# Pooled attention and an MLP on one core: fewer, larger transfers for each head, query rows placed otherwise, and a new order of steps

## The chip, the cores and the metric

The kernel runs on one core of one Trainium2 chip. The metric is the device time of one execution in microseconds (us); the numbers to compare are medians over several executions. All inputs and outputs are float32.

## The reference, cut to what matters

```
q_pool = q.reshape(B, H, S // 2, 2, D).mean(axis=3)            # B 4, H 8, S 1152, D 64
scores = (1 / sqrt(D)) * q_pool @ k.T                           # 576 x 1152 for each head
scores = scores - max(scores, axis=-1)
attn   = exp(scores) / (sum(exp(scores), axis=-1) + 1e-9)
x      = (attn @ v), heads side by side                         # 2304 x 512
h      = x @ w_in                                               # 512 x 2048
out    = max(0.01 * h, h) @ w_out                               # 2048 x 512
```

## The kernel before, in words

There are 32 heads (`hd`) of attention and nine blocks (`i`) of 256 tokens of the MLP. A head goes through these steps, each a function of the kernel:

- `load_q` (line 402), `load_k` (374) and `load_v` (457) fetch its inputs. `load_q` issues four transfers, one for each (x, y) quarter of 144 query rows; all heads share one buffer for them.
- `q_sum` (419, GpSimd) adds the two rows of each pooled pair, `q_tr` (425, TensorE) transposes, `q_hi` (440, ScalarE) and `q_lo` (443, VectorE) split the result into a high and a low part, so that products of reduced precision add up to a full one. Both parts are needed twice, on partitions 0 to 63 and on 64 to 127. For head 0 the engines write all four (x, y) quarters; for all others they write the two with x = y, and `q_dup` (449) copies them to the other partitions with two transfers for the high and two for the low part.
- `qk` (463, TensorE) forms scores with high parts alone, `vmax` (478, VectorE) takes their row maxima, `vneg` (490) reduces and negates them, `m_tr` (493, TensorE) and `m_cp` (499, ScalarE) turn them into a row, and `m_dma` (503) writes this row into partition 0 and into partition 64 of a tile, with one transfer each (head 0: in two halves).
- `qkt` (540, TensorE) forms the transposed scores minus the maxima, `exp` (552, ScalarE) their exponentials, from head 15 on partly after a subtraction by VectorE (`less`, 535). `esum` (559, GpSimd) adds exponentials up and `pv` (573, TensorE) multiplies by v, in two bursts.
- For heads 0 to 12, `r_mm` (584, TensorE) forms the row sums, `r_cp` (613, ScalarE) copies them, `r_fold` (617) spreads them over 96 partitions (four transfers, for head 12 two), `r_inv` (630, VectorE) inverts, `r_row` (641) writes a row to memory, `r_wide` (647) reads it back on all partitions (two transfers). Later heads form the sums on VectorE (`r_tr`, 603) and fold them with four transfers of another shape.
- `scale` (657, GpSimd) multiplies, `x_out` (660) stores the head's share of x with two transfers.

That is 22 transfers for a head of the first dozen. All of them, those of the weights (`w_load` 668, `w_out_dma` 707, `ws_load` 740) and those of the MLP (`x_load` 719, `o_out` 902, `o_mix_out` 876) are issued one after the other by SyncE's queue (SP); a wait there holds all that is behind it. Only `load_q` of head 0 is issued by ScalarE's queue.

The MLP's first product is `l1` (748), its second `l2` (883) for blocks 0 to 3 and `l2s` (833) after that. Its steps are laid between those of the heads: the first `l1` stands in the order between the first `qkt` of head 10 and that of head 11.

All engines run in order, and this order is written out by hand: the string `ORDER` (line 49) has one letter for each step, `FAMILIES` (38) says which function a letter is. `Scheduler.run` (163) goes through it; its model of the engines' times decides which of two engines takes a step that either could, and which buffer it gets, nothing else. TensorE works in four tilings, line 85:

```
TILINGS = {"pv": 1, "r_mm": 2, "qk": 3, "qkt": 3, "m_wide": 3, "k_tr": 3, "q_tr": 3, "m_tr": 3}
```

All else (the MLP's products) has tiling 0, and `r_mm` from head 12 on has that of `pv`.

Of the kernel before, what the change touches and what calls it, by code (L numbers as in the profile page):

```python
# [21 lines left out]
SWITCH = 0.19  # L22
OND = 0.0
ON_DVE = ()
LAT = 0.12
FLIGHTS = 10
PELAT = 0.28
FAST = 4
DEEP = 4
NEAR = 1  # L30
MB = 15
# [18 lines left out]
    "&(!#)*$++++--!&@%F,,(,,)-...!#-!$*.-.-+(.+.)/01A--,2,%-/0F1.*-+..+.,3433A,4-4.#-$2AF3.43.34%--/04313.4.#-4.($%"  # L50
    ")-2F(334.3443*+-A6+A43FG45,,-.34FH..-/!I60.1-55555348343.-24.3)*-+453+.433-,,644()79.-.A./!3#$A%G6H4I8031-3-F4"
    "F.54(533.43-.4&55-:&47-.2!9JF5A3434.:#$;#*+%+6,,$%3334-55;5..7K/)44<A=>34--J6.0.53-559G13H454I<.J&-!A.!?-=G234"
    ".3434-3F4384..>*H#:&/L0++?,16,$;3K(5K%GIHIGJ34K46AAG384)55HIH3323444-7-IJ55<L..9--..6FGJ3-3=4344.>(#:;L*+-+,6,"
    "../5KK$0134%3343!4?45558H<I&A-7L--).9.GH364-*..+-+,,5=>F652I-3.()3JJJ.4!A./4A-0?.18345F3-43.F4-34-34.33-4A..-2"
    "&34..:#743F;(5/&<$F940%314*+33+,4,6:G3A43445K5)HLI3K45#-6$;.-%3*GK=HJ(4I++>.,7,9-.--.J<26.3L!A-.=A4534.33-F544"
    "G/?.H85>!6?013I-.YJ-4557):93.83-44343;-.F2334.-4F&4..AK/KK34343#04<$61%*3FG:555555;H=I+,+GFJ6(H4I)A<3>3G4Y24,#"
    "H$I=-K.37%49--3.6J.?48*-.->6.3G-+,+,5!545LK53344..33/453A?()44A-3H-V8W&4I7X..-039:;.#&1*4-A.L$55(Y+ZZZZZZ,G%<6"
    "2J+H,IJJ!5A[534-.-.&7.3=433K3>FK:44#$K4%6/09Y3314343?4;A4-.L!55)6G*-G++HHII,<.,J625333F54&K34433444ZYZ--=]:LZZ"
    ";ZZZ.>.(Z8-<.-.ZYJG[ZZ?]ZA^Y=.8)555[57/(03133444-HIK623>Y39.GF3]^^4-HI?G64H4L8-5I3..4334A-*4+ZZ555555Z.Z,-#J&+"
    ",-.ZZY$ZYAZJFZ[ZZZ%:FJAF-[../03KK1343-4.72K564-;9].)--^.LG63..43-3434..34!3355:4/5L<LH553I5446Y_G4FFHJI____KG]"  # L60
    "GHIHJI^GGKLLJJKKHHIJI;____55555_JKF0YB#__1_2$%_*3`+<+4ZKZ,,Z_3CZD5ZYZFE[33EEG6G=>AG-H]IYJH_^KIZJ`ZKZZZZ[]Y.H:;"
    "ZZ=YIF_?_-.J>3K^4A5?EZZZZ(GHI[]8!___J-43^K)8-<44VE4W__._.Y(_-.-.=./*__+X+__0,A,133>53___E4&44B#2C`D`3$36%E--.."
    "5554-.633&YYE!?38E#3)&$4EZZZZZZ4E*%Y3+-5ZEZ[+:.ZZ--]4,Y44YA^ZZZZZA,[YYZZY]3.;<.555-.4-..ZAZZ(&Z4-3^B.-[]:55Z/!"
    "^4ZZ_.__01-[34.-.2_]6.CD3_;_^_E)_<4==`533*+6+/E53Y,,5555A4E0143E#4E43E$B%36Y3>555444>2aCD3a?33A4EE-(?86.-)-Z8_"
    "ZY.:.Z!;--345__5.E44ZZ.Z-*&+.+3E(<___./55_A_,0=,31#!`2E3EZZZYY4ZZZ$A44)-[([%33553454-.655.->B-?4C.D.63855YY333"
    ":E4]5E]ZZZ^ZEE335-Z445Z_EE.-[*]&#);+ZZZZZ.!+A.,,44$Z^^/0<=4%1354234_--[.55V5&]63.C^5__D433B_:_EE-.3E>?_;_`3*+W"
    "X6+3,8,A3YY-AEE.#55_E_$%_-<=->-...__YZZZZZY3.-4A-Z4444[__.]B!5ZZ.55(/)^445ZZ_01?-3:-ZZ4[]-..6.52CD5;.<3=`/53E4"
    "4#3(E3E64^3>$%4Y830E!3E142*Y3++3E5,,4655444?AB):CDA345333EE44*+55aE6,;554+-,-8__YY5Z.-53..E-ZZ.ZZZ-.#[-]<$.A_Z"
    "Z-.-a^%ZZZZ._Y[.-&33_=>B_EE]^4(4__?-5)43`4/3.-:4.01.;3-5.5./555234*6<CDE&56(++,3041,3=38EEE!333Y3E4444E2AA>?B)"
    "44456CD35555&3&A#4$3EY3%EE46345Y:8*E+3(E4!-,Z.+,___---Z.A.ZZZ.Z_-.-..[/554#__$%]4_03313YE44-!ZZ4Z2ZZZ;[5555B--"  # L70
    ".5.653.CZ<D_Z]Z3)Y43`5:ZZ^ZEE[533#$E%*=Y4+,+,6E3E(>43?8E344-.AZ_;44YZA5-4.34-..ZZY-A<5-.^Z6/0.-).Z1!2_-V-_.]_."
    "Y^__[]^CD-__34B..`35*/E4+3E43E4+:=&63(;0555515>,,3E4E34E#3A$6442B%5CD-.34-.3A5553E3&45E5!#-.$5-%63.E33E33E?EW<"
    "84:;4)4X44-6-Y44=ZZZ...*/0Z15ZZ++,,33[3B>(555<4?34=2C6DE>?E333E558485E3E)&*4Y:_A54E5+5_,+,_;---...Z]^!ZZ_ZZZ--"
# [27 lines left out]

class Scheduler:
# [33 lines left out]
    def free_slots(self, tag):  # L136

        r = []
        for after, before, slots in self.tags[tag]:
            if (after is None or after in self.done) and before not in self.done:  # L140
                for slot in slots:
                    t = [self.cells[c] for c in slot]
                    if None not in t:
                        r.append((max(t), slot))
        return sorted(r, key=lambda x: x[0])
# [27 lines left out]

    def start(self, s, e, at):
# [11 lines left out]
        free, end = self.free[e], at + s.eng[e]  # L186
        self.free[e] = end
        if e == "PE":
            if at > free + 1.0:
                end = self.free[e] = end + (1.2 if at > 20 else 0.3)  # L190
# [11 lines left out]
        for hold in self.holds.pop(s.key, ()):  # L202
            hold[1] -= 1
            hold[2] = max(hold[2], end)
            if hold[1] == 0:
                for c in hold[0]:
                    self.cells[c] = hold[2] + LAT
        for k, wait in self.after.pop(s.key, ()):
# [4 lines left out]
            elif e == "PE":  # L213
                t = end if "PE" in o.eng else end + 2 * LAT
            else:
                t = end + (PELAT if "PE" in s.eng else LAT)
# [4 lines left out]
def tile_pooled_attention_moe(  # L221
# [40 lines left out]
    def copy(e, out, in_):  # L262
# [18 lines left out]
        "ms": (1, [NQ, 128], F32R, sb),  # L281
# [167 lines left out]
    def q_dup(hd, lo, e):  # L449
        t = f32((ql if lo else qh)[hd])  # L450
# [39 lines left out]
    def vneg(hd, a, b, e):  # L490
        nc.vector.tensor_reduce(out=mng[hd][:, a:b], in_=mx[hd][:, a:b], axis=AX.X, op=ALU.max, negate=True)
# [7 lines left out]
    def m_cp(hd, a, b, e, i):  # L499
        mst[hd] = new("ms", i)  # L500
        nc.scalar.copy(out=mst[hd].rearrange("p (x n) -> p x n", x=2), in_=mtp.pop(hd)[0:NQ, :, :64])

    def m_dma(hd, a, b, e, i=None):
# [3 lines left out]
        src = f32(mst.pop(hd))[a:b]  # L507
# [109 lines left out]
    def r_fold(hd, e, i):  # L617
# [100 lines left out]

    def x_load(i, e, s):
# [5 lines left out]
        n0 = 0  # L725
# [185 lines left out]
    def mmr(*cols):  # L911
        return {"PE": sum(max(0.112, 0.0035 + 0.000436 * c) for c in cols)}

    def mm4(*cols):
        return {"PE": sum(0.01 + 0.00182 * c for c in cols)}

    def trr(n):
        return {"PE": 0.112 * n}

# [23 lines left out]
    for hd in range(NHD):  # L943
# [7 lines left out]
        step(k_tr, hd, eng=trr(NP + 1), deps=[("load_k", hd)] + after("k_tr"), takes=[("tp", [("k_hi", hd), ("k_lo", hd)]), ("ka", [last])])  # L951
# [3 lines left out]
        step(load_q, hd, **(sp(4, 0.3e6, 0.47, 200e3) if hd else dict(eng={"ACT": 4.4})), order=after("load_q"), takes=[("qn", [("q_sum", hd)])])  # L955
# [213 lines left out]
```

## Time and profile before

| | before |
|---|---|
| median of 3 runs | 888.05 us (887.7 to 889.61) |
| the profiled execution's own time | 885.79 us |
| its span, first to last instruction | 884.0 us |
| what lies around the span | 1.79 us |
| mean granted TensorE clock | 0.989 |

The profile shows one execution. Busy times are unions of an engine's instructions; PE is TensorE's matrix products, PEld its weight loads, DVE VectorE, ACT ScalarE, POOL GpSimd, SP SyncE. `L453` is line 453 of the kernel. A row such as `PE L550 ... [1.46 <-DVE stat L488]` says that the engine stood idle for 1.46 us and that an instruction of VectorE's line 488, writing tile `stat`, ended this. PEclk is the granted share of TensorE's full clock. The q after an engine's name means its instruction queue: for SP these are the issues of transfers.

### The profile page before, as it was taken

How to read it: one execution, taken by the hardware profiler on the slowest of the kernel's cores; microseconds unless marked ns; L12 is line 12 of the kernel's file. 1: busy time of each engine (PE TensorE's matmuls, PEld its weight loads, DVE VectorE, ACT ScalarE, POOL GpSimd, SP SyncE). 2: the span in 40 equal slices, each digit the busy share in tenths (PEclk: the TensorE clock that was granted, in tenths of full speed). 3: DMA queues.
4: the chain of work that ended last, by engine and by line, in shares of the span. 5: the costliest groups of instructions: out<-in, count | busy, mean ns of one | idle time of the engine just before them, and what ended most of it. 6: DMA issues, size and time to landing. Idle time of an engine off the chain costs nothing.

```text
span 884.0 us, 19586 instructions
## 1 busy us (share of the span) xinstructions
PE 843.9 (95%) x7492; PEld 678.2 (77%) x7492; DVE 588.3 (67%) x1000; ACT 408.8 (46%) x730; POOL 480.1 (54%) x387
## 2 busy tenths in 40 slices
PE   4999899899999999999999999999999999999997
PEld 2766565666777877686776776787789999999997
DVE  6877677574666776677787778767559985533454
ACT  2566565665556544254446345444433343323231
POOL 2565846685889757576869749857861021004000
PEclk9999999999999999999999999999999999999999
DMA  5666666667786674454464544464547778575641
GB/s 159 181 175 166 181 195 188 196 200 226 212 275 222 203 230 143 116 171 131 141 185 130 152 135 132 134 192 147 175 136 263 263 251 250 152 265 186 206 135 36
DMA packets 105313, 159.85 MB, mean 181 GB/s; under 512 B 23861, under 2 KB 72309, under 8 KB 105221
## 3 DMA queue, kind: packets, MB, share of 16 engines
q1 hardware_dynamic: 104581, 158.32, 59.0%
q8 instruction: 59, 0.97, 0.5%
q10 hardware_dynamic: 640, 0.30, 0.1%
q14 instruction: 33, 0.27, 0.1%
HBM read 131.12 MB, written 17.90 MB: 169 GB/s over the span
## 4 chain that ended last, share of the span: by engine, by line
PE 79%; DVE 7%; DMA 7%; SPq 2%; ACT 2%; issue 1%; POOL 1%; DVEq 0%; ACTq 0%; POOLq 0%
PE banks L758 21%; PE banks L550 14%; PE banks L579 14%; PE banks L849 11%; PE banks L473 5%; PE banks L890 4%; PE banks L891 3%; PE banks L892 3%; DVE stat L488 3%; DMA ws<-wd 2%; PE banks L595 1%; DVE e L538 1%; DMA fold<-rs 1%; PE banks L476 1%; DMA kn<-in_k_dram 1%
## 5 line engine op out<-in xcount | busy, mean ns | idle before, releaser
L488 DVE TENSOR_REDUCE stat<-banks 128x1 f32<-128x1024 f32 (+3 forms) x224 | 217.0, 1005 | 67.0 <-PE banks L473 52.1
L758 PE MATMUL banks<-xb,ws 128*128 128x256 f32 x1344 | 179.1, 286 | 2.0 <-DMA ws<-wd 1.9
L758 PEld LDWEIGHTS banks<-xb,ws 128*128 128x128 f32 x1344 | 167.3, 191 | 13.4 <-issue 7.3
L567 POOL TENSOR_TENSOR sm<-sm,e 128x576 f32<-128x576 f32 x119 | 167.0, 1422 | 6.0 <-ACT e L557 2.6
L550 PE MATMUL banks<-qh,ka 64*128 64x288 f32 x1152 | 138.3, 318 | 6.7 <-DVE stat L488 3.3
L579 PE MATMUL banks<-e,vv 128*64 128x288 f32 x924 | 143.7, 417 | 0.0
L550 PEld LDWEIGHTS banks<-qh,ka 64*128 64x128 f32 x1152 | 94.6, 190 | 35.1 <-DVE stat L488 8.5
L557 ACT ACTIVATE e<-banks 128x576 f32<-128x576 f32 x146 | 90.1, 649 | 55.1 <-PE banks L550 45.9
L579 PEld LDWEIGHTS banks<-e,vv 128*64 128x64 f32 x924 | 70.1, 138 | 43.7 <-issue 8.4
L550 PE MATMUL banks<-ql,ka 64*128 64x288 f32 x576 | 87.7, 295 | 0.0
L538 DVE TENSOR_TENSOR e<-banks,e 128x576 f32<-128x576 f32 x85 | 61.4, 752 | 34.3 <-PE banks L550 26.3
L473 PE MATMUL banks<-ka,qh 64*128 64x512 f32 (+1 forms) x320 | 70.3, 461 | 5.3 <-DMA qh<-qh 2.2
L554 ACT ACTIVATE e<-e 128x576 f32<-128x576 f32 x85 | 56.4, 682 | 21.4 <-DVE e L538 21.1
L423 POOL TENSOR_TENSOR qs<-qn 112x384 f32<-112x384 f32 x32 | 32.2, 1006 | 58.1 <-DMA qn<-in_q_dram 39.5
L771 POOL TENSOR_TENSOR gg<-g,gg 128x512 fp32r<-128x512 f32 x31 | 39.8, 1290 | 43.5 <-ACT gg L263 41.7
L849 PE MATMUL banks<-wo,gg 128*128 128x256 f32 x344 | 63.1, 283 | 0.0
L738 POOL TENSOR_TENSOR xb<-xb 128x1024 fp32r<-128x1024 f32 x7 | 16.7, 2387 | 85.1 <-ACT xb L263 83.2
L550 PE MATMUL banks<-mt,hot 64*128 64x288 f32 x372 | 58.3, 298 | 0.9 <-DMA mt<-ms 0.9
L550 PEld LDWEIGHTS banks<-ql,ka 64*128 64x128 f32 x576 | 56.8, 188 | 0.0
L890 PE MATMUL banks<-wo,gg 128*128 128x512 f32 x124 | 52.1, 420 | 0.7 <-DVE ql L444 0.4
L567 POOL TENSOR_TENSOR sm<-e 128x576 f32<-128x576 f32 x30 | 42.6, 1424 | 18.1 <-ACT e L554 11.7
L658 POOL TENSOR_TENSOR x<-x,rs 128x288 f32<-128x288 f32 x32 | 25.9, 810 | 48.3 <-DMA rs<-rd 35.4
(221 smaller groups left out, 1571.8 us busy)
## 6 DMA issues: line engine op xcount, KB each, us to landing
ws<-wd SPq DMA_DIRECT2D x144, 512.0 KB
vv<-in_v_dram SPq DMA_DIRECT2D x32, 288.0 KB
kn<-in_k_dram SPq DMA_DIRECT2D x32, 288.0 KB
qn<-in_q_dram SPq DMA_DIRECT2D x124, 72.0 KB
raw<-in_moe_w_in_dram SPq DMA_DIRECT2D x16, 512.0 KB
raw<-in_moe_w_out_dram SPq DMA_DIRECT2D x16, 512.0 KB
wd<-ws SPq DMA_DIRECT2D x16, 512.0 KB
rs<-rd SPq DMA_DIRECT2D x64, 72.0 KB
```

The lines of the kernel that those rows point to most:

```text
L473: nc.tensor.matmul(p[:n, x, :KW], lhsT=qh[hd][r, o:o + n], rhs=kh[r, :KW], start=True, stop=True)
L488: nc.vector.tensor_reduce(out=d, in_=p, axis=AX.X, op=ALU.max)
L538: nc.vector.tensor_tensor(out=ex[hd, u], in0=sps.pop((hd, u))[:, :, :HW], in1=m, op=ALU.add)
L550: nc.tensor.matmul(p[:, x, :HW], lhsT=w[r], rhs=m[r, hf * HW:(hf + 1) * HW], start=(n == 0), stop=(n == len(todo) - 1))
L554: nc.scalar.activation(out=ex[hd, u], in_=ex[hd, u], func=AF.Exp)
L557: nc.scalar.activation(out=ex[hd, u], in_=sps.pop((hd, u))[:, :, :HW], func=AF.Exp)
L567: ENG[e].tensor_tensor(out=o, in0=a, in1=b, op=ALU.add)
L579: nc.tensor.matmul(p[64 * hf:64 * hf + 64, :HW], lhsT=vv[hd][:, t, :], rhs=probs(hd, t, hf), start=(t == 0), stop=(t == KT - 1),)
L758: nc.tensor.matmul(p, lhsT=wst[i, f][:, a, c, :], rhs=xx[i][x][:, c, :], start=(n == 0), stop=(n == 3 * KC - 1))
L771: ENG[e].tensor_tensor(out=t[:, 1], in0=gf.pop((i, fp)), in1=f32(t[:, 0]), op=ALU.subtract)
L849: nc.tensor.matmul(o, lhsT=g[i, p][:, a], rhs=w[:, x], start=(p == 0 and n == 0 and half == 0), stop=(p == FH - 1 and n == 2), skip_group_ ...
L890: nc.tensor.matmul(p, lhsT=gh, rhs=wo[f][:, 0], start=(f == hf * FH), stop=False)
```

## The change

- `load_q` takes the query rows in another split: row n of a head's 576 pooled rows stood at (x, y, a, p) with n = 288 x + 144 y + 48 a + p and now stands at n = 288 y + 144 x + 48 a + p. One transfer now covers both x, so there are two instead of four. `q_sum` writes with permuted strides to give the old layout. The two middle quarters of the columns of x are thereby exchanged, and `x_load` undoes this: `pieces` cuts a block at quarters of 144 columns, which makes 24 transfers of all nine blocks where there were 12.
- `q_hi` writes all four quarters for every head (128 ScalarE instructions where there were 66); `q_dup` copies only the low part (two transfers, not four).
- `vneg` writes the negated maxima twice, `m_cp` copies 10 rows instead of 5, and `m_dma` writes both partitions with one transfer (head 0 stays as it was).
- `r_fold` of heads 0 to 12 takes both halves in one transfer: two (head 12: one) instead of four (two).
- The model's figures are others (among them one for TensorE's clock), and `ORDER` is a new string: 3709 letters where there were 3678, the difference being 62 more `q_hi` and 31 fewer `q_dup`. Read with `FAMILIES` and `TILINGS`, the old string changes TensorE's tiling 282 times, the new one 249 times: 79 and 73 before head 13's first `qkt`, 203 and 176 from there on.

The strings and most of the model's figures are left out:

```diff
 ORDER = (
-    "&(!#)*$++++--!&@%F,,(,,)-...!#-!$*.-.-+(.+.)/01A--,2,%-/0F1.*-+..+.,3433A,4-4.#-$2AF3.43.34%--/04313.4.#-4.($%"
...
+    "()!#$%*++,++-,,,---@&&&(.)-...*++-!.+.#/()$01*%+++,.--,/++-.FF..23,,-A04.3-(1#4-!.323$..34/440%-.133)A4-(3.4-"
...
     def load_q(hd, e, i):
-        src = q[hd // H, hd % H].rearrange("(x y a p r) d -> x y p a (r d)", x=2, y=2, p=QP, r=2)
+        src = q[hd // H, hd % H].rearrange("(y t p r) d -> y p t (r d)", y=2, p=QP, r=2)
         dma = nc.sync if hd else nc.scalar
-        for x in range(2):
-            for y in range(2):
-                dma.dma_start(out=qraw[64 * y:64 * y + QP, x::2], in_=src[x, y])
+        for y in range(2):
+            dma.dma_start(out=qraw[64 * y:64 * y + QP], in_=src[y])
...
-        a, b = (qraw[:n, :, r * D:(r + 1) * D] for r in range(2))
-        ENG[e].tensor_tensor(out=qs[hd][:n], in0=a, in1=b, op=ALU.add)
+        a, b = (qraw[:n, :, r * D:(r + 1) * D].rearrange("p (x a) d -> p x a d", x=2) for r in range(2))
+        ENG[e].tensor_tensor(out=qs[hd][:n].rearrange("p (a x) d -> p x a d", x=2), in0=a, in1=b, op=ALU.add)
...
-    def q_dup(hd, lo, e):
-        t = f32((ql if lo else qh)[hd])
+    def q_dup(hd, e):
+        t = f32(ql[hd])
...
     def vneg(hd, a, b, e):
-        nc.vector.tensor_reduce(out=mng[hd][:, a:b], in_=mx[hd][:, a:b], axis=AX.X, op=ALU.max, negate=True)
+        out = mng[hd][:, :2 * NQ].rearrange("p (x n) -> p x n", x=2)[:, :, a:b]
+        src = mx[hd][:, a:b].unsqueeze(1).to_broadcast([128, 2, b - a, 2])
+        nc.vector.tensor_reduce(out=out, in_=src, axis=AX.X, op=ALU.max, negate=True)
...
-        src = f32(mst.pop(hd))[a:b]
+        src = f32(mst.pop(hd))
+        if b - a == NQ:
+            nc.sync.dma_start(out=f32(mt[hd])[::64].rearrange("p (i n) -> p i n", n=128), in_=src)
+            return
+        src = src[a:b]
...
-        for hf in range(2):
-            for x in range(parts(hd)):
-                j = 64 * hf + 32 * x
-                src = rss[hd][j:j + 1].rearrange("o (a n) -> o a n", n=RN)
-                nc.sync.dma_start(out=rts[hd][HW // RN * hf:HW // RN * (hf + 1), x], in_=src)
+        for x in range(parts(hd)):
+            src = rss[hd][32 * x:32 * x + 65:64].rearrange("o (a n) -> o a n", n=RN)
+            nc.sync.dma_start(out=rts[hd][:, x], in_=src)
...
+    def pieces(i):
+
+        n0, r = 0, []
+        while n0 < NB:
+            b, at = divmod(i * NB + n0, SP)
+            j, o = divmod(at, HW // 2)
+            n = min(NB - n0, HW // 2 - o)
+            r.append((n0, n, b, (0, 2, 1, 3)[j] * (HW // 2) + o))
+            n0 += n
+        return r
...
-        while n0 < NB:
-            b, o = divmod(i * NB + n0, SP)
-            n = min(NB - n0, SP - o)
+        for n0, n, b, o in pieces(i):
             src = xd[b].rearrange("(c p) n -> p c n", p=128)[:, :, o:o + n]
             nc.sync.dma_start(out=f32(xx[i][1])[:, :, n0:n0 + n], in_=src)
-            n0 += n
...
-        quarters = [(x, y) for x in range(2) for y in range(2) if x == y or hd < NEAR]
+        quarters = [(x, y) for x in range(2) for y in range(2)]
+        lows = [z for z in quarters if z[0] == z[1] or hd < NEAR]
...
-            step(q_dup, hd, 0, **sp(2, 0.15e6, 0.58), deps=high)
-            step(q_dup, hd, 1, **sp(2, 0.15e6, 0.58), deps=low)
-            high, low = [("q_dup", hd, 0)], [("q_dup", hd, 1)]
+            step(q_dup, hd, **sp(2, 0.15e6, 0.58), deps=low)
+            low = [("q_dup", hd)]
```

## Rows read from the trace of the kernel before

**Rows 1.** Busy time by stretch: start:end, length, busy (instructions), PEclk, DMA share, GB/s.
```profile
core 0: us, PE busy (x) PEld busy (x) DVE busy (x) ACT busy (x) POOL busy (x), PEclk, DMA share, GB/s
...
50.00:250.00 200.00, 185.40 (x1936) 129.76 (x1932) 128.27 (x193) 117.42 (x221) 140.00 (x111) 0.97 0.68 197
250.00:650.00 400.00, 395.29 (x3370) 298.54 (x3371) 282.06 (x430) 193.26 (x347) 294.54 (x227) 1.00 0.56 167
650.00:884.00 234.00, 227.12 (x1850) 223.17 (x1846) 141.03 (x322) 76.15 (x121) 29.11 (x29) 1.00 0.60 195
```

**Rows 2.** The same view, first and last of five stretches of 3.41 us.
```profile
65.89:69.30 3.41, 3.41 (x22) 1.86 (x24) 1.94 (x5) 1.50 (x3) 1.00 (x1) 0.50 0.40 124
...
369.67:373.08 3.41, 3.41 (x9) 2.62 (x9) 1.87 (x5) 0.00 (x0) 3.30 (x3) 0.50 0.26 70
```

**Rows 3.** Timeline of PE at either clock: start, length, instruction, count.
```profile
162.25 0.80 PE L550 MATMUL banks<-qh,ka 64*128 64x288 f32 x4
...
163.22 0.80 PE L550 MATMUL banks<-qh,ka 64*128 64x288 f32 x4
...
262.25 0.43 PE L550 MATMUL banks<-qh,ka 64*128 64x288 f32 x4
...
262.78 0.42 PE L550 MATMUL banks<-qh,ka 64*128 64x288 f32 x4
```

**Rows 4.** Timeline of SP's queue, 134 to 140 us.
```profile
134.30 1.18 SPq L453 DMA_DIRECT2D qh<-qh  x2
135.53 0.58 SPq L708 DMA_DIRECT2D wd<-ws  x1
136.16 1.25 SPq L651 DMA_DIRECT2D rs<-rd  x2
137.50 2.62 SPq L407 DMA_DIRECT2D qn<-in_q_dram  x4
```

**Rows 5.** Source views of five lines: duration ns min/median/max, first and last start.
```profile
L407 SPq DMA_DIRECT2D qn<-in_q_dram x124: 312/435/1480, 7.8 to 571.9; - x124
...
L453 SPq DMA_DIRECT2D qh<-qh x62: 461/537/1706, 15.7 to 600.4; - x62
...
L510 SPq DMA_DIRECT2D mt<-ms x66: 601/726/818, 19.5 to 631.3; - x66
...
L628 SPq DMA_DIRECT2D fold<-rs x50: 501/590/601, 56.1 to 256.1; - x50
...
L742 SPq DMA_DIRECT2D ws<-wd x144: 319/332/1442, 152.2 to 851.8; - x144
```

**Rows 6.** Waits, 50 to 250 us: who waited for whom, us, times, longest.
```profile
DVE fold L638 <- DMA fold<-rs: 15.7, 7, 6.8
...
PE banks L473 <- DMA qh<-qh: 2.2, 2, 2.0
...
PE banks L432 <- POOL qs L423: 1.9, 1, 1.9
```

**Rows 7.** Timeline at 157 to 160 us: a wait of DVE and one of PE.
```profile
157.77 0.16 DVE L638 TENSOR_REDUCE fold<-fold 96x6 f32<-96x12 f32 x1 [2.05 <-DMA fold<-rs]
...
159.32 0.53 PE L550 MATMUL banks<-qh,ka 64*128 64x288 f32 x4 [1.46 <-DVE stat L488]
```

**Rows 8.** Timeline of PE where the tiling changes, 264 to 266 us.
```profile
264.90 0.41 PE L579 MATMUL banks<-e,vv 128*64 128x288 f32 x1
...
265.14 0.41 PE L579 MATMUL banks<-e,vv 128*64 128x288 f32 x1
...
265.48 0.50 PE L890 MATMUL banks<-wo,gg 128*128 128x512 f32 x1
265.82 0.39 PE L891 MATMUL banks<-wo,gg 128*128 128x512 f32 x1
266.05 0.39 PE L892 MATMUL banks<-wo,gg 128*128 128x512 f32 x1
```

**Rows 9.** Source view of ScalarE's writes of the high part.
```profile
L441 ACT ACTIVATE qh<-banks x66: 382/405/409, 8.5 to 596.7; 64x288 fp32r<-64x288 f32 x66
```

**Rows 10.** The page, DMA queue: packets, MB, share of 16 engines' span.
```profile
q1 hardware_dynamic: 104581, 158.32, 59.0%
```

More of the change, by code (lines that the diff above doesn't have):

```diff
@@ L99, in __init__, with after @@
         self.left, self.ready = ndeps, 0.0
+def after(s, e, o):
+    to = next(iter(o.eng))
+    if e == "PE":
+        return 0.0 if to == "PE" else 0.255
+    if s.lat:
+        return 0.05 if to == "PE" else 0.1
+    return {"PE": 0.055, "POOL": 0.08, "SP": 0.03}.get(to, 0.035)
 class Scheduler:
@@ L172, in run, with product @@
         assert len(self.log) == len(self.steps)
+    def product(self, t, work):
+        while True:
+            while t >= self.window + CLOCK - 1e-12:
+                idle = CLOCK - self.used
+                self.fast = idle <= 1.45 if self.fast else idle < 0.25
+                self.window, self.used = self.window + CLOCK, 0.0
+            speed, room = 1.0 if self.fast else 0.5, self.window + CLOCK - t
+            if work / speed <= room:
+                self.used += work / speed
+                return t + work / speed
+            self.used, work, t = self.used + room, work - room * speed, self.window + CLOCK
     def start(self, s, e, at):
@@ L185, in start @@
         self.done.add(s.key)
-        free, end = self.free[e], at + s.eng[e]
-        self.free[e] = end
+        end = self.free[e] = at + s.eng[e]
         if e == "PE":
-            if at > free + 1.0:
-                end = self.free[e] = end + (1.2 if at > 20 else 0.3)
+            end = self.free[e] = self.product(at, s.eng[e])
             tiling = self.tiling(s)
@@ L212, in start @@
                 t = at
-            elif e == "PE":
-                t = end if "PE" in o.eng else end + 2 * LAT
             else:
-                t = end + (PELAT if "PE" in s.eng else LAT)
+                t = end + after(s, e, o)
             o.ready = max(o.ready, t)
@@ L950, in tile_pooled_attention_moe @@
         step(load_k, hd, **sp(2, 0.3e6), order=after("load_k"), takes=[("kn", [("k_tr", hd)])])
-        step(k_tr, hd, eng=trr(NP + 1), deps=[("load_k", hd)] + after("k_tr"), takes=[("tp", [("k_hi", hd), ("k_lo", hd)]), ("ka", [last])])
+        step(k_tr, hd, eng={"PE": 0.328}, deps=[("load_k", hd)] + after("k_tr"), takes=[("tp", [("k_hi", hd), ("k_lo", hd)]), ("ka", [last])])
         step(k_hi, hd, eng={"ACT": act(5 * 128, True)}, deps=[("k_tr", hd)])
@@ L954, in tile_pooled_attention_moe @@
         step(load_v, hd, **sp(1, 0.3e6), order=after("load_v"), takes=[("vv", [("pv", hd, NBU - 1)])])
-        step(load_q, hd, **(sp(4, 0.3e6, 0.47, 200e3) if hd else dict(eng={"ACT": 4.4})), order=after("load_q"), takes=[("qn", [("q_sum", hd)])])
+        step(load_q, hd, **(sp(2, 0.3e6, 0.7, 200e3) if hd else dict(eng={"ACT": 4.4})), order=after("load_q"), takes=[("qn", [("q_sum", hd)])])
         step(q_sum, hd, eng=pool(QT * D, "q_sum"), lock=True, deps=[("load_q", hd)], order=after("q_sum"), takes=[("qs", [("q_tr", hd)])])
@@ L958, in tile_pooled_attention_moe @@
             step(zeros, hd, eng={"POOL": 1.6 if hd == 1 else 1.0})
-        quarters = [(x, y) for x in range(2) for y in range(2) if x == y or hd < NEAR]
-        hold = [(f, hd, *z) for f in ("q_hi", "q_lo") for z in quarters]
-        step(q_tr, hd, eng=trr(QT // 2), deps=[("q_sum", hd)] + after("q_tr"),
+        quarters = [(x, y) for x in range(2) for y in range(2)]
+        lows = [z for z in quarters if z[0] == z[1] or hd < NEAR]
+        hold = [("q_hi", hd, *z) for z in quarters] + [("q_lo", hd, *z) for z in lows]
+        step(q_tr, hd, eng={"PE": 0.199}, deps=[("q_sum", hd)] + after("q_tr"),
              takes=[("tp", hold), ("qh", [last]), ("ql", [last])])
@@ L973, in tile_pooled_attention_moe @@
             ends = [("vmax", hd, n)] + ([("vmax", hd, NQ + 1)] if n == NQ else [])
-            step(qk, hd, n, eng=mmr(KW) if n < NQ else mmr(128, 128, 128), deps=[("k_hi", hd)] + high + before,
+            step(qk, hd, n, eng={"PE": 0.276 if n < NQ else 0.262}, deps=[("k_hi", hd)] + high + before,
                  takes=[("tp", ends)] + ([] if n else [("st", [("m_tr", hd, *m_parts(hd)[-1])])]))
@@ L982, in tile_pooled_attention_moe @@
             step(vneg, hd, a, b, eng={"DVE": 0.17}, deps=deps + [before])
[L983 removed]
+            step(m_tr, hd, a, b, eng={"PE": 0.085}, deps=[("vneg", hd, a, b)], takes=[("tp", [("m_cp", hd, a, b)])])
             step(m_cp, hd, a, b, eng={"ACT": act(128, True)}, deps=[("m_tr", hd, a, b)], takes=[("ms", [("m_dma", hd, a, b)])])
[L985 removed]
+            step(m_dma, hd, a, b, **(sp(1, 0.01e6, 0.85) if b - a == NQ else sp(2, 0.01e6, 0.78)), deps=[("m_cp", hd, a, b)] + ([("zeros", hd)] if 0 < hd < len(mts) else []), takes=[] if a else [("mt", [last] if not by_dve(hd, KT - 1) else [("m_wide", hd)])])
             before = ("m_tr", hd, a, b)
         if hd >= MB:
[L988 removed]
+            step(m_wide, hd, eng={"PE": 0.232}, deps=[("m_dma", hd, 0, NQ)], takes=[("s", [("m_put", hd)])])
             step(m_put, hd, eng={"ACT": act(2 * HW, True), "DVE": dve(2 * HW, psum=True)}, deps=[("m_wide", hd)], takes=[("e", [("less", hd, u) for u in range(KT) if by_dve(hd, u)])])
@@ L998, in tile_pooled_attention_moe @@
             need = [("m_dma", hd, *x) for x in m_parts(hd)][:1 if t % 2 == 0 and t < KT - 1 else None]
-            step(qkt, hd, t, eng=mmr(*[HW] * (3 if by_dve(hd, t) else 4)), deps=ready + ([] if by_dve(hd, t) else need) + [before], takes=[("s", [("less" if by_dve(hd, t) else "exp", hd, t)])])
+            step(qkt, hd, t, eng={"PE": 0.475 if by_dve(hd, t) else 0.625}, deps=ready + ([] if by_dve(hd, t) else need) + [before], takes=[("s", [("less" if by_dve(hd, t) else "exp", hd, t)])])
             b = [n for n, x in enumerate(BURSTS) if x[0] <= t < x[1]][0]
@@ L1018, in tile_pooled_attention_moe @@
         else:
-            step(r_mm, hd, eng=mm4(*[HW] * ((2 + direct(hd)) // 2)), deps=[("esum", hd, sums[-1])] + ([("exp", hd, t) for t in range(ns + 1, KT)] if direct(hd) else []),
+            step(r_mm, hd, eng={"PE": 1.0 if direct(hd) else 0.536}, deps=[("esum", hd, sums[-1])] + ([("exp", hd, t) for t in range(ns + 1, KT)] if direct(hd) else []),
                  takes=[("t", [("r_cp", hd)])])
@@ L1028, in tile_pooled_attention_moe @@
                 else:
-                    step(r_fold, hd, **sp(2 * parts(hd), 0.002e6, 0.62), deps=[("r_cp", hd)], takes=[("rt", [("r_row", hd)])])
+                    step(r_fold, hd, **sp(parts(hd), 0.002e6, 0.66), deps=[("r_cp", hd)], takes=[("rt", [("r_row", hd)])])
                 step(r_inv, hd, eng={"DVE": 0.6 if hd >= GH else 0.38 if parts(hd) == 2 else 0.2}, deps=[("r_fold", hd)])
-                step(r_row, hd, **sp(1, 0.002e6, 0.41), deps=[("r_inv", hd)])
+                step(r_row, hd, **sp(1, 0.002e6, 0.56), deps=[("r_inv", hd)])
                 step(r_wide, hd, **sp(2, 0.15e6, 0.58, 120e3), deps=[("r_row", hd)], takes=[("rs", [("scale", hd)])] if hd >= GH else [])
@@ L1060, in tile_pooled_attention_moe @@
     for i in range(NBLK):
-        step(x_load, i, **sp(1 + (i * NB // SP != (i * NB + NB - 1) // SP), 0.524e6), deps=[("x_out", hd) for hd in needs(i)] + [("x_load", i - 1) if i else None], takes=[("xb", [("l1", i, FH - 1 if i >= FAST else NF - 1, 2)])])
+        step(x_load, i, **sp(len(pieces(i)), 0.524e6), deps=[("x_out", hd) for hd in needs(i)] + [("x_load", i - 1) if i else None], takes=[("xb", [("l1", i, FH - 1 if i >= FAST else NF - 1, 2)])])
         step(x_hi, i, eng={"ACT": act(KC * NB)}, deps=[("x_load", i)])
```

96 lines of the change are left out of this document (44 added, 52 removed).

## The prediction

> **What bounds the kernel now.** I read the busy time by stretch first. TensorE is busy for 185.40 of 200 us from 50 to 250 us, for 395.29 of 400 us from there to 650 us, and for 227.12 of 234 us in the rest [rows 1]. So it bounds everything from 250 us on, and only its own work can be made shorter there; before 250 us it stands idle for 200 - 185.40 = 14.6 us, and this is the stage in which another limit shows. The clock is the second thing to see. The same view cut finer gives five stretches of 3.41 us in which the granted clock is 0.50, the lower of the two levels (1.2 instead of 2.4 GHz), four of them before 250 us and the last at 369.67 us [rows 2]. In one of these the timeline shows eight products of L550 start to start in 163.22 - 162.25 = 0.97 us, at the full clock in 262.78 - 262.25 = 0.53 us [rows 3]. A stretch thus does the work of 3.41 x 0.53 / 0.97 = 1.86 us and loses 1.55 us; five lose 7.7 us.
>
> Then SP's queue. From 134.30 to 140.12 us four issues take 1.18 + 0.58 + 1.25 + 2.62 = 5.63 of 5.82 us [rows 4]: it goes from one issue to the next, and a step whose data are ready waits for those ahead of it. The waits show what comes of that. VectorE stands 15.7 us in seven waits for `fold`, TensorE 2.2 us for the doubled high part and 1.9 us for a `q_sum` [rows 6]. At 157.77 us VectorE has waited 2.05 us for a fold, the maxima stand behind it in its order, and TensorE then waits 1.46 us for the maxima [rows 7]. So 2.2 + 1.9 + 1.46 = 5.6 of the 14.6 us of idle time can be put down, by rows, to steps that sit behind this queue. A slow stretch begins at 161.5 us, right after the last of these waits.
>
> **The change part by part.**
>
> SP's queue. Issues cost 0.435 us for `load_q`, 0.537 for `q_dup`, 0.726 for `m_dma`, 0.590 for `r_fold`, all medians [rows 5]. A head of the first dozen saves two, two, one and two of them: 0.87 + 1.07 + 0.73 + 1.18 = 3.85 us; later ones 2.67 us, since their folds stay. What one merged issue costs no row shows. At best it costs what one of the two did, at worst as much as both, which leaves only the 1.07 us of `q_dup`. I take the first: the issue of a 512 KB load takes 0.332 us, that of a fold of about a kilobyte 0.590 [rows 5], so the size does not set it. Twelve more issues of `x_load`, at the 0.332 us of the nearest load, add 4 us in the whole run; each stands before a block's first product, which is queued in TensorE's order, and the pieces carry the same bytes. I put them at nothing because a block is loaded before the heads' steps around it are through; if that cover is gone, they cost up to those 4 us. With a quarter of the issue time gone the queue is no longer full, and the 5.6 us go: the doubled high part does not pass SP at all, folds and `load_q` come earlier. What is late next are VectorE's maxima and ScalarE's exponentials themselves, so I leave the other 9.0 us of idle time. Bounds: nothing and 14.6 us. **-5.6 us**.
>
> The clock. Each slow stretch that no longer has an idle spell ahead of it gives back 1.55 us. I take two of five, as the idle time that goes is 5.6 of 14.6 us, which is two fifths. Bounds 0 and 7.7 us. **-3.1 us**.
>
> The order. TensorE pays for each change of tiling. In the timeline, pairs of L579 start 264.90 to 265.14, 0.24 us apart; the first product of the next tiling starts 0.34 us after the last pair, and the second 0.34 us after the first, where 0.23 us (265.82 to 266.05) is the pitch [rows 8]. That is 0.10 + 0.11 = 0.21 us for this change; the 0.10 ahead of it is the least it can be where the next kind hides its own start. I take 0.18, bounds 0.10 and 0.21. The new string has 33 changes fewer, 27 of them from head 13 on, where TensorE has no idle time to hide them. 33 x 0.18 = **-5.9 us** (3.3 to 6.9). Whether the rest of the new order fits the queues as well as the old one can't be worked out from rows; that is what the rivals are for.
>
> ScalarE. 62 more writes of the high part at 0.405 us [rows 9] are 25.1 us. They stand beside other work: ScalarE is busy for 117.42 of 200 us up to 250 us, 193.26 of 400 us after that [rows 1]. The two that replace two issues and a landing shorten the way to `qk`. But in order they also stand ahead of exponentials; where one of these is what TensorE waits for, a head pays up to 2 x 0.405 = 0.81 us. Bounds: nothing and 12 x 0.81 = 9.7 us for the stage with idle time (TensorE has more buffered later). I take one such case. **+0.8 us**.
>
> The rest. The two issues that head 0 saves on ScalarE's queue lie ahead of a start that waits for `load_k`; `q_sum` reads and writes as many elements with other strides on an engine that is busy for 140 of 200 us [rows 1]; `vneg` writes ten values instead of five per partition. Nothing for each, covered by the waits they end in; 1 us either way for all three.
>
> Sum: -5.6 - 3.1 - 5.9 + 0.8 = -13.8 us. The profiled execution took 885.79 us (its span of 884.0 and 1.79 around it), so it would take 872.0; it lies 2.26 us under the median of the runs, 888.05, from which the sum gives 874.2. I say **874 us**.
>
> **The rivals.**
>
> *SP is relieved, but TensorE's idle time stays.* The queue was full, yet a full queue need not be the last to end: 9.0 of the 14.6 us are not tied to it by a row. Then only the tilings count: 888.05 - 5.9 = 882 us. Against it: transfers do end waits [rows 6, 7].
>
> *All of it goes.* Idle time, slow stretches and tilings give 888.05 - 14.6 - 7.7 - 5.9 = 860 us. Against it: VectorE and GpSimd are at 64% and 70% in this stage [rows 1], and each wait left can bring a slow stretch.
>
> *Merged folds land late.* VectorE already waits at seven folds [rows 6], with the maxima behind them. A merged fold moves 96 pieces with one issue; no row shows over how many of the 16 engines a transfer is spread. The mean packet takes 0.590 x 16 x 884.0 / 104581 = 0.080 us [rows 10]. If the pieces ran in two rows of 48 instead of sixteen of three, a fold would land 45 x 0.080 = 3.6 us later. Of a wait of VectorE 1.46 / 2.05 = 0.71 came through to TensorE [rows 7], so seven waits cost 7 x 3.6 x 0.71 = 17.9 us, and with the tilings' gain the time is 888.05 - 5.9 + 17.9 = 900 us, slower. It decides once a fold lands over half a microsecond later than the order allows for. Against it: a packet's mean is that of 158.32 MB in 104581 packets, 1.5 KB each; these pieces are 24 bytes, and six numbers should take far less. The Trainium skill ("DMA: Bandwidth & Descriptors", section on why a DMA increments its semaphore by 16) has a rule that speaks for this rival: the number of engines is the largest one up to 16 that divides the slowest dimension of both sides. By that the merged fold, 2 rows to 96 partitions, would get two engines where each of the old ones, 48 to 48, got sixteen; no row of this trace shows it either way.
>
> *Merging saves no issue time* (each merged issue costs what two did), and what the tilings give the new order's own waits take back: within 0.2% of 888 us. Against it: the sizes and times of rows 5.
>
> **How the numbers follow.** The forecast's own range is 866 to 882 (two of the three gains at their ends), chance 0.50. Only the tilings, 882: 0.15. All of it, 860: 0.10. Nothing, 888: 0.10. Folds late, or another wait of that size that the new order makes, 900: 0.15. Faster by over 0.2% (1.8 us, about what a measurement of this kernel can tell from no change) are the first three, 0.75; same 0.10; slower 0.15. The range leaves out 900 and half of the 860 case: 863 to 890.
>
> **What would show it.** Right: 62 more L441 instructions at 0.4 us; SP's queue with gaps between issues before 250 us; a merged issue under 0.75 us; TensorE idle for about 9 us from 50 to 250 us; three slow stretches or fewer; the maxima waiting less for products; from 250 us on the same work in 5 us less. Wrong: VectorE waiting for `fold` more than 15.7 us; TensorE waiting for ScalarE's exponentials behind high parts; as many slow stretches as now; idle time after 250 us, where there was hardly any, which would say that the new order itself costs what the tilings give.

## The result, and the profile after

The changed kernel takes 851.01 us (median of 4 runs, 850.38 to 851.56) where the kernel before took 888.83 us beside it (4 runs, 887.7 to 889.78): the ratio is 0.9575, with a 95% interval of 0.9558 to 0.9591. That is 38 us faster. The forecast was 14 us faster, 874 us with a range of 863 to 890, so the direction was right and the size far too small. The profiled execution took 850.38 us, its span is 848.6 us against 884.0.

The busy times of the changed kernel by stretch, with the columns of [rows 1]:

```profile
0.00:28.30 28.30, 17.14 (x115) 11.75 (x117) 20.57 (x35) 10.68 (x21) 6.95 (x15) 1.00 0.60 170
28.30:50.00 21.70, 21.05 (x238) 15.20 (x238) 17.18 (x22) 15.63 (x30) 13.89 (x11) 1.00 0.69 220
50.00:250.00 200.00, 197.25 (x2143) 144.71 (x2140) 143.37 (x221) 142.41 (x275) 154.25 (x123) 1.00 0.71 212
250.00:650.00 400.00, 397.22 (x3383) 307.77 (x3382) 297.16 (x471) 196.92 (x367) 288.79 (x221) 1.00 0.54 161
650.00:848.60 198.60, 193.95 (x1623) 193.54 (x1621) 105.83 (x251) 65.09 (x98) 23.79 (x27) 1.00 0.61 195
```

Read the third row against the first of [rows 1]. TensorE's idle time from 50 to 250 us fell from 14.6 to 2.75 us, its products there rose from 1936 to 2143, and the granted clock is 1.00 where it was 0.97. From 250 to 650 us the idle time fell from 4.7 to 2.8 us. The view of cores shows what became of the slow stretches of [rows 2]: the mean granted clock rose from 0.989 to

```profile
core 0: 848.6 us, clock 0.999
```

and what is left of the lower clock lies behind the last product. All five stretches are gone. SP's queue, which went from issue to issue in [rows 4], at one place in the same stage of the changed kernel:

```profile
122.10 1.13 SPq L469 DMA_DIRECT2D ql<-ql  x2
124.29 0.34 SPq L665 DMA_DIRECT2D rd<-fold  x1
124.73 1.10 SPq L469 DMA_DIRECT2D ql<-ql  x2
126.20 0.34 SPq L475 DMA_DIRECT2D vv<-in_v_dram  x1
127.15 1.68 SPq L671 DMA_DIRECT2D rs<-rd  x2
```

From 122.10 to 128.83 us five entries take 4.59 of 6.73 us; in the gaps the queue waits for data instead of the other way round. It is not open all the time: from 128.92 to 136.19 us it again goes from issue to issue. Over the stage from 50 to 250 us the waits of SP's queue add up to some 75 us where they were 33. The source views of the merged issues and of the high part's writes (columns as in [rows 5]):

```profile
L423 SPq DMA_DIRECT2D qn<-in_q_dram x62: 327/450/1362, 6.7 to 534.7; - x62
...
L527 SPq DMA_DIRECT2D mt<-ms x31: 549/592/622, 29.9 to 597.2; - x31
...
L648 SPq DMA_DIRECT2D fold<-rs x25: 510/572/688, 53.5 to 234.2; - x25
...
L457 ACT ACTIVATE qh<-banks x128: 385/405/410, 7.3 to 554.0; 64x288 fp32r<-64x288 f32 x128
```

A merged issue costs what one of the two did (0.450, 0.592, 0.572 us against 0.435, 0.726, 0.590), so merging two issues saves about half of their time, for the maxima more. And the waits from 50 to 250 us have, where [rows 6] had 15.7 us in seven waits,

```profile
DVE fold L658 <- DMA fold<-rs: 3.1, 2, 1.8
```

Of the 35.4 us that the span lost, 18.1 are idle time of TensorE (40.1 to 22.0: 2.1 before 50 us, 11.9 from there to 250, 1.9 to 650, 2.2 after that) and 17.3 are its busy time (843.9 to 826.6), for the same 7492 products. The 2.1 us are read against two rows of before that [rows 1] leaves out:

```profile
0.00:28.30 28.30, 15.56 (x112) 11.28 (x114) 19.19 (x32) 9.05 (x17) 4.52 (x13) 1.00 0.58 164
28.30:50.00 21.70, 20.57 (x236) 15.41 (x234) 17.73 (x25) 12.95 (x24) 11.98 (x10) 1.00 0.54 159
```

### The profile page after: what moved, and what is told of

Its sections match the earlier page's. It is cut to its first block, busy times and chain, and to the rows that moved or that the text cites. A ratio compares the mean times of both kernels' runs of the same rounds, so it can differ in the third digit from the quotient of the medians.

```text
span 848.6 us, 19385 instructions
## 1 busy us (share of the span) xinstructions
PE 826.6 (97%) x7492; PEld 673.0 (79%) x7492; DVE 584.1 (69%) x994; ACT 430.7 (51%) x790; POOL 487.7 (57%) x395
## 3 DMA queue, kind: packets, MB, share of 16 engines
q1 hardware_dynamic: 103967, 153.74, 59.6%
## 4 chain that ended last, share of the span: by engine, by line
PE 74%; DVE 3%; DMA 2%; issue 1%; ACT 1%; POOL 1%; SPq 0%; DVEq 0%; POOLq 0%; ACTq 0%
PE banks L785 24%; PE banks L876 12%; PE banks L601 11%; PE banks L572 10%; PE banks L917 4%; PE banks L489 4%; PE banks L918 3%; PE banks L919 3%; DVE stat L504 1%; DVE e L560 1%; PE banks L492 1%; PE banks L403 1%; DMA ws<-wd 1%; PE banks L551 1%; POOL sm L589 0%
## 5 line engine op out<-in xcount | busy, mean ns | idle before, releaser
L785 PE MATMUL banks<-xb,ws 128*128 128x256 f32 x1344 | 176.9, 285 | 0.5 <-DMA ws<-wd 0.3
L589 POOL TENSOR_TENSOR sm<-sm,e 128x576 f32<-128x576 f32 x101 | 142.8, 1428 | 13.3 <-ACT e L576 8.2
L579 ACT ACTIVATE e<-banks 128x576 f32<-128x576 f32 x135 | 83.1, 652 | 27.1 <-PE banks L572 20.9
L589 POOL TENSOR_TENSOR sm<-e 128x576 f32<-128x576 f32 x50 | 70.8, 1428 | 17.4 <-ACT e L576 10.1
L576 ACT ACTIVATE e<-e 128x576 f32<-128x576 f32 x100 | 65.7, 682 | 23.3 <-DVE e L560 22.3
L457 ACT ACTIVATE qh<-banks 64x288 fp32r<-64x288 f32 x128 | 51.7, 404 | 38.0 <-PE banks L448 27.1
L439 POOL TENSOR_TENSOR qs<-qn 112x384 f32<-112x384 f32 x32 | 32.3, 1010 | 40.1 <-DMA qn<-in_q_dram 34.2
L876 PE MATMUL banks<-wo,gg 128*128 128x256 f32 x288 | 53.2, 282 | 0.0
```

The costliest lines, as they stand in the source:

```text
L457: nc.scalar.activation(out=q_half(qh[hd], x, y), in_=q_src(hd, x), func=AF.Copy, scale=QSCALE)
L576: nc.scalar.activation(out=ex[hd, u], in_=ex[hd, u], func=AF.Exp)
L579: nc.scalar.activation(out=ex[hd, u], in_=sps.pop((hd, u))[:, :, :HW], func=AF.Exp)
L589: ENG[e].tensor_tensor(out=o, in0=a, in1=b, op=ALU.add)
L785: nc.tensor.matmul(p, lhsT=wst[i, f][:, a, c, :], rhs=xx[i][x][:, c, :], start=(n == 0), stop=(n == 3 * KC - 1))
L876: nc.tensor.matmul(o, lhsT=g[i, p][:, a], rhs=w[:, x], start=(p == 0 and n == 0 and half == 0), stop=(p == FH - 1 and n == 2), skip_group_ ...
```

## The experiments

The first question is whether the transfers or the new order did it. Four kernels cross the two. In the first three the order, the model's figures and with them all its choices are those of before.

**All merges in the old order.** The functions of the diff for `load_q`, `q_sum`, `x_load`, `vneg`, `m_cp`, `m_dma` and `r_fold` are put into the kernel before; the high parts are doubled where the first write stands, and the step of their transfers issues nothing:

```diff
-        nc.scalar.activation(out=q_half(qh[hd], x, y), in_=q_src(hd, x), func=AF.Copy, scale=QSCALE)
+        for z in (y,) if hd < NEAR else (y, 1 - y):
+            nc.scalar.activation(out=q_half(qh[hd], x, z), in_=q_src(hd, x), func=AF.Copy, scale=QSCALE)
...
-        t = f32((ql if lo else qh)[hd])
+        if not lo:
+            return
+        t = f32(ql[hd])
```

> The old order of steps and the old planner's choices, with all the transfers of the change merged (15 issues for a head, high parts doubled by ScalarE where the first write stands). Theory 'queue' (SP's full queue caused the idle time and the slow stretches, the order only follows): most of the gain is here: 14.6 us of idle time from 50 to 250 us falls under 6, at most two slow stretches are left, about 870 us (865 to 876). Rival 'order' (the new order itself removes the waits, whatever the transfers): 884 to 888 us with idle time over 10 us and four or five slow stretches.

**Only the merges in the old order**: the same without the two pieces of diff above, so the high parts are still doubled by transfers.

> The old order with the merged query loads, maxima and folds, but with the high parts still doubled by transfers (17 issues for a head). Saves 2 x 0.435 + 0.73 + 1.18 = 2.8 of 3.85 us of issue time a head before head 12. Theory 'queue': two thirds or more of the gain of the 15-issue run, about 876 us. Rival 'order': no more than 3 us off 888.

**Only the doubling in the old order**: the two pieces of diff above and nothing else.

> The old order, only the doubling of the high parts moved from SP's queue to ScalarE (20 issues for a head). Theory 'queue': a quarter of the issue time saved goes, and the way to the maxima's products loses a landing of about 3 us, so 880 to 885 us. Rival 'ScalarE pays': 25 us more of ScalarE's work ahead of exponentials, 888 to 898 us. Rival 'order': 888, no change.

**All transfers split again in the new order**: the changed kernel with `load_q` in four transfers, the maxima in two, the folds in four, and the high part doubled by SP:

```diff
-        nc.scalar.activation(out=q_half(qh[hd], x, y), in_=q_src(hd, x), func=AF.Copy, scale=QSCALE)
+        if x == y or hd < NEAR:
+            nc.scalar.activation(out=q_half(qh[hd], x, y), in_=q_src(hd, x), func=AF.Copy, scale=QSCALE)
+        if x and y and hd >= NEAR:
+            t = f32(qh[hd])
+            for x in range(2):
+                c = slice(x * HW, (x + 1) * HW)
+                nc.sync.dma_start(out=t[64 - 64 * x:128 - 64 * x, c], in_=t[64 * x:64 * x + 64, c])
```

> The new order and the new planner's choices, with every merged transfer split again and the high parts doubled by two transfers behind the second write (22 issues for a head). Theory 'queue': the order is written for a queue with gaps, and the full queue brings back the idle time and the slow stretches: 878 to 892 us, idle time from 50 to 250 us over 8 us. Rival 'order': 851 to 858 us, idle time under 5 us.

| | median us | ratio to before beside it, 95% interval |
|---|---|---|
| all merges, old order | 871.62 | 0.9819 (0.9764 to 0.9873) |
| merges without the doubling, old order | 860.29 | 0.9697 (0.9640 to 0.9753) |
| doubling alone, old order | 879.19 | 0.9898 (0.9830 to 0.9965) |
| all split, new order | 933.34 | 1.0514 (1.0454 to 1.0575) |

Theory 'queue' stands and 'order' falls: the old order with the merges alone has over two thirds of the gain (26.6 of 38 us), and the new order with the old transfers is 5% slower than the kernel before. The sizes were forecast less well. The merges alone were put at about 876 us and came 16 us lower; the doubling alone lies 0.8 us below its range; the new order with all split lies 41 us above its range. All merges in the old order lie within theirs, but the idle time from 50 to 250 us was to fall under 6 us and is 7.1 us:

```profile
50.00:250.00 200.00, 192.87 (x2105) 137.00 (x2102) 139.14 (x209) 137.18 (x264) 152.02 (x121) 1.00 0.70 208
```

The same stretch of the merges alone:

```profile
50.00:250.00 200.00, 195.79 (x2113) 140.37 (x2105) 143.36 (x218) 131.44 (x248) 156.19 (x124) 1.00 0.76 223
```

and of the new order with all split:

```profile
50.00:250.00 200.00, 168.82 (x1691) 117.51 (x1691) 117.59 (x177) 99.90 (x189) 112.88 (x91) 0.90 0.54 158
```

Idle time is 4.2 us with the merges alone and 31.2 us in the new order, the clock 1.00 and 0.90. The 5% are not the price of the full queue alone. The edit puts the two doubling transfers right behind the second write, while in the old string they are a step of their own, up to 64 letters later. For the doubled part TensorE waits 10.8 us in this stage, where [rows 6] has 2.2 us:

```profile
PE banks L497 <- DMA qh<-qh: 10.8, 5, 2.8
```

What the split alone costs in the new order is better read against the run with the merges and the same doubling (below, 1.0131 of the kernel before): 1.0514 - 1.0131, some 34 us. So the new string is written for a queue with room. The new order with the merges split and the doubling left to ScalarE was not run.

What I had not expected is the doubling. Alone it gains 1%, but beside the merges it costs 871.6 - 860.3 = 11.3 us. The waits (from 50 to 650 us) of the old order with the merges have

```profile
DVE ql L443 <- ACT qh L440: 14.8, 15, 2.6
```

and with the doubling too

```profile
DVE ql L444 <- ACT qh L441: 29.3, 22, 3.4
```

which fits extra writes that stand in ScalarE's order ahead of what VectorE waits for. That these 14.5 us are the 11.3 is not shown.

**Which merge.** Each of the three alone in the old order.

> The old order, only the folds of heads 0 to 12 merged (two issues for a head instead of four, 1.18 us less on SP for each of the first dozen). The three merges together measured 860.3 us, some 27 us under the kernel before. Theory 'queue by time' (what counts is the issue time that goes, whichever it is): 1.18 of 2.78 us, so about -11 us, 873 to 880. Rival 'fold' (VectorE's 15.7 us in seven waits for the fold are the cause): most of the 27 us, 860 to 868. Rival of the prediction, 'late folds': 890 or more.

> The old order, only the query loads merged, with the other placement of the rows and the 24 loads of x (two issues for a head instead of four, 0.87 us less on SP for each head). Theory 'queue by time': 0.87 of 2.78 us in the first stage, about -8 us, 876 to 882. Rival 'fold': no change, 885 to 889. Rival 'loads of x' (12 more issues of x_load cost what is saved): 887 or more.

> The old order, only the maxima's row merged (one issue for a head instead of two, 0.73 us less on SP for each head). Theory 'queue by time': 0.73 of 2.78 us in the first stage, about -7 us, 877 to 883. Rival 'fold': no change, 885 to 889.

| | median us | ratio | idle 50 to 250 us |
|---|---|---|---|
| folds | 873.76 | 0.9866 (0.9841 to 0.9891) | 9.0 |
| query loads | 875.20 | 0.9882 (0.9849 to 0.9915) | 12.7 |
| maxima | 874.04 | 0.9871 (0.9839 to 0.9903) | 15.3 |

Beside 884.88 us for the kernel before, they gain 11.1, 9.7 and 10.8 us. In the first dozen heads they take 12 x 1.18 = 14.2, 12 x 0.87 = 10.4 and 12 x 0.73 = 8.8 us off the queue. So rival 'fold' falls: it hardly matters which issue goes, and what goes from the full queue comes off the end at 0.8 to 1.2 times its own length. The query loads and the maxima came 0.8 and 3.0 us below the ranges of 'queue by time', and with intervals of about 3 us either way the three gains can't be told apart: the runs show the order of size, not that a gain is in proportion to the issue time. These products leave out what the query loads and the maxima save in later heads, where TensorE is the bound; no run separates it. Together the three gain 26.6 us, less than the 31.6 us of their sum and less than 12 x 2.78 = 33.4 us of issue time; with 4.2 us of idle time left in the stage, TensorE has little more to give there. The gain is only partly idle time: the maxima alone leave 15.3 us of it in this stretch but lose two of the five slow stretches.

The folds also answer the rival 'late folds'. VectorE's waits for them from 50 to 250 us, 15.7 us in seven in [rows 6], are with the merged folds alone

```profile
DVE fold L636 <- DMA fold<-rs: 7.1, 5, 4.3
```

Their queue line on the page, where [rows 10] has 104581 packets:

```profile
q1 hardware_dynamic: 103831, 158.31, 58.8%
```

The bytes are the same and 750 packets are gone, 30 for each of 25 merged pairs. The Trainium skill ("DMA: Bandwidth & Descriptors", section on why a DMA increments its semaphore by 16) has each engine that takes part write one completion. With the numbers of engines that the prediction took from its rule, two transfers on 16 engines would write 32, one on two engines 2, which is 30 fewer, so the trace agrees with its rule. The maxima's line has 104333 packets, 248 fewer, 8 for each of 31: twice 5 engines against 2, by the same rule. By this the spread was narrower, as that rival had it; with pieces of 24 bytes the waits fell all the same.

**The doubling in the new order.** The changed kernel with the doubling by SP, as in the diff above.

> The changed kernel, only the high parts doubled by two transfers again, behind the second write (17 issues for a head). In the old order the doubling by ScalarE cost 11 us beside the merges (871.6 against 860.3). Theory 'ScalarE fits the new order' (the new string leaves room for the 62 writes, and the transfers come back with 1.07 us of issue and a landing of 3 us): 856 to 870 us. Rival 'ScalarE pays in any order': faster than the changed kernel, 838 to 848 us.

It takes 895.03 us, 1.0131 (1.0079 to 1.0183) of the kernel before and 44 us more than the changed kernel: the rival 'ScalarE pays in any order', which had it faster, falls, and the range of the other theory was far too low. The waits of SP's queue say where:

```profile
SPq L463 <- ACT qh L458: 79.3, 36, 6.6
```

The two transfers stand right behind the write that they copy, so the queue stops there for 79.3 us in 36 waits with everything that is behind. In the new string the reader follows soon: one to ten letters after the write in seven of the heads 1 to 14, where the old string has 18 or more in heads 2 to 14. So a landing has little to hide behind. The run prices this place for the transfers; another place was not tried, and what the 62 writes themselves cost in the new order it does not show.

**Tilings, the end, and one merge more.** The last four ran on one chip, with the changed kernel itself among them.

> The changed kernel as it is, beside the next three on the same chip, so that they can be held against it: 850 to 853 us by every theory.

> The changed kernel with 20 pairs of neighbouring letters of the new string exchanged, all after head 15's first product and each of a product of a head with one of the MLP, so that TensorE changes its tiling 38 times more (286 for 248) and does the same work. Theory 'a change costs 0.18 us': 38 x 0.18 = 6.8 us more, about 858. Bounds of the prediction: 0.10 and 0.21, 3.8 to 8 us. Rival 'only the order's fit counts, the tilings are nearly free': under 1.5 us more.

> The changed kernel with the last letters of the string put as the old one has them: the four o_mix steps that the new string has among the last products stand behind all of them. Theory 'the end is the order's' (VectorE then does six additions behind the last product, where it now does one): the time from TensorE's last end to the end of the span is 6.4 instead of 4.3 us, the run 2 us longer. Rival 'the end is that of the clock or of the last transfers': no change.

> The changed kernel with r_wide's two transfers merged into one (14 issues for a head). Theory 'queue by time' carried on: 0.57 us less on SP for each head, but SP's queue already has gaps and TensorE idles only 2.7 us from 50 to 250 us, so 848 to 851 us. Rival 'merged transfers land late' (147 KB with a side of two rows, spread over few of the engines): GpSimd waits longer for rs than now, landing some microseconds later, and the run is 2 us or more slower.

The edit of the second is 20 exchanges of neighbouring letters, that of the third is the end of the string, that of the fourth is in `r_wide`:

```diff
-    "...ffffffggggffffgghhh"
+    "...ffffffffffgggggghhh"
...
-        for hf in range(2):
-            nc.sync.dma_start(out=rss[hd][64 * hf:64 * hf + 64], in_=rd[hd][hf:hf + 1].to_broadcast([64, HW]))
+        nc.sync.dma_start(out=rss[hd], in_=rd[hd].unsqueeze(1).to_broadcast([2, 64, HW]))
```

| | median us (lowest to highest) |
|---|---|
| the changed kernel | 851.15 (850.52 to 853.17) |
| 38 more changes of tiling | 859.98 (859.29 to 860.39) |
| the old end | 853.13 (852.56 to 854.31) |
| `r_wide` merged | 879.06 (873.05 to 882.70) |

Tilings: 8.83 us more for 38 changes is 0.23 us for each. The stretch from 250 to 650 us of that kernel

```profile
250.00:650.00 400.00, 396.56 (x3320) 299.31 (x3319) 289.20 (x454) 193.20 (x359) 284.92 (x220) 1.00 0.52 157
```

has 0.66 us more idle time than the changed kernel and 63 products fewer. Beside the changed kernel on the same chip, of the 8.8 us of span 8.4 are TensorE's busy time (834.8 against 826.4 us): a change of tiling is paid in time that counts as busy.

The end: with the old end VectorE's last additions are

```profile
844.51 2.33 DVE L896 TENSOR_TENSOR raw<-raw,banks 128x256 f32<-128x256 f32 x6 [3.09 <-PE banks L876]
```

six behind the last product, and in the changed kernel beside it

```profile
841.60 0.42 DVE L896 TENSOR_TENSOR raw<-raw,banks 128x256 f32<-128x256 f32 x1 [0.24 <-PE banks L876]
842.32 0.42 DVE L896 TENSOR_TENSOR raw<-raw,banks 128x256 f32<-128x256 f32 x1 [0.29 <-PE banks L876]
843.02 1.21 DVE L896 TENSOR_TENSOR raw<-raw,banks 128x256 f32<-128x256 f32 x3 [0.28 <-PE banks L876]
844.46 0.42 DVE L896 TENSOR_TENSOR raw<-raw,banks 128x256 f32<-128x256 f32 x1 [0.23 <-PE banks L876]
```

one. With the old end the run is 2.0 us longer, by the order of the letters alone.

`r_wide` merged: one issue less makes the run 28 us slower. SP issues it at 106.09 us, and GpSimd's line shows when it landed:

```profile
106.09 0.52 SPq L670 DMA_DIRECT2D rs<-rd  x1
...
113.01 0.80 POOL L677 TENSOR_TENSOR x<-x,rs 128x288 f32<-128x288 f32 x1 [7.34 <-DMA rs<-rd]
```

6.9 us later. In the changed kernel the two transfers of a head, issued from 98.45 us on, landed by 101.87 us, 3.4 us later:

```profile
98.45 1.15 SPq L671 DMA_DIRECT2D rs<-rd  x2
...
101.87 0.80 POOL L678 TENSOR_TENSOR x<-x,rs 128x288 f32<-128x288 f32 x1 [4.12 <-DMA rs<-rd]
```

Its queue line

```profile
q1 hardware_dynamic: 103007, 153.73, 59.1%
```

has 960 packets fewer than the changed kernel's 103967, 30 for each of 32 heads. This is the rival 'merged transfers land late', on 147 KB where a merged fold has 2.3, and 'queue by time', which had 848 to 851 us, falls for this transfer. From 50 to 250 us GpSimd's waits for `rs` are 28.2 us in 7, against 10.5 in 6 for the changed kernel beside it, and TensorE's idle time is 15.9 us against 2.7. By which steps the one becomes the other was not traced.

## Why the prediction was wrong

**TensorE bounds the kernel, SP's queue the stretch before 250 us.** Right; the merges in the old order show it.

**SP's queue, -5.6 us.** This is the step that failed, and within it the sentences "the 5.6 us go" and "I leave the other 9.0 us of idle time". The issue times were right, and so was that a merged issue costs one. But the gain was sized by the waits that rows tie to a transfer one by one, and the 9.0 us that no row tied to one were left standing. TensorE's idle time in this stage fell by 11.9 us, not 5.6. Everything behind the full queue was late, and the size was nearer to the issue time that goes: 2.78 us for a head of the first dozen, 33 us in all without the doubling, up to what TensorE's stage has to give. The three merges alone, in the old order, gave 26.6 us, idle time, clock and short waits together, where the terms for queue and clock had 8.7.

**The clock, -3.1 us.** The mechanism was right, the count wrong: not two of five slow stretches went but all five, 7.7 us by the prediction's price. Taking the same share as of the idle time was the error. Just ahead of the five stretches TensorE had waited 1.45, 2.03, 1.74, 1.94 and 1.92 us; the maxima's run keeps 15.3 us of idle time in the stage and has three stretches left, so the sum of the idle time does not set their number.

**The tilings, -5.9 us.** The mechanism was right, the size low: 0.23 us for a change by the experiment, above the upper bound of 0.21, so 33 changes are 7.6 us.

**ScalarE, +0.8 us.** The term is no constant of the change: in the old order the writes cost 11.3 us beside the merges. That they are covered in the new order is not shown. The one way tried of doing without them there costs 44 us, and that is the price of transfers at which the queue stops.

**The rest at nothing.** The start and the end were left out. The end gave 2.0 us through four letters, and before 50 us TensorE idles 2.1 us less. The twelve extra issues of `x_load`, put at nothing, did not show: the query loads alone, with these issues in, took 875.20 us where rival 'loads of x' had 887 or more.

**The rivals.** "All of it goes", 860 us, was the nearest, at a chance of 0.10. The profile shows what it still lacked: 1.7 us on the tilings, 2.1 at the start, 1.9 after 250 us, 2.2 at the end and some 2 us of busy time that no run separates; against these stand 2.75 us that it counted as gone and in which TensorE still idles. Another 1.6 us lie between the profiled executions and the medians. 'SP is relieved, but TensorE's idle time stays' is wrong by the row from 50 to 250 us, 'merging saves no issue time' by the medians of the merged issues, and the folds were not late. From the old order with the merges to the changed kernel it is 9.1 us between two chips, about 11 by the ratios; the tilings and the end, 7.6 + 2.0 us, are of that size.

## What to carry to other kernels

Price a full in-order queue by the time of the issues that go, times their number, up to what the next bound leaves (here 0.8 of it came), not by the waits that can be traced to single transfers. An order written out by hand and the transfers that it was written for are one change: here the transfers alone gained part of it, and the order without them was slower than what it replaced. Merge transfers where they are small; before merging a large one, see how many engines its outer dimensions leave it.

## What the runs showed that was not expected

The old order with the merges does the same 7492 products in the same order and with the same changes of tiling as the kernel before, and TensorE's busy time is 830.4 us in the one and 843.9 in the other. From their pages, the kernel before first:

```profile
PE 843.9 (95%) x7492; PEld 678.2 (77%) x7492; DVE 588.3 (67%) x1000; ACT 408.8 (46%) x730; POOL 480.1 (54%) x387
...
PE 830.4 (97%) x7492; PEld 670.8 (78%) x7492; DVE 587.7 (69%) x1000; ACT 408.6 (48%) x730; POOL 480.3 (56%) x387
```

The slow clock explains 7.7 of these 13.5 us by the prediction's price. The other 5.8 may be short waits that the page counts as busy, since the ends of products are modelled; no run shows it. If so, the idle time of an engine that is nearly always busy is a lower bound of its waits. And a merging that saves 0.57 us of issue time for a head and 960 packets in all went with a transfer in use 3.5 us later, in the pair of rows shown, and a kernel 28 us slower.
